# Go-ahead products issued one at a time, the last expert's rows of x2 two steps sooner, sigmoid's table loaded by itself, and two planner costs

## The chip, the cores and the metric

The kernel runs on one core of a Trainium2 chip. The metric is the device time of one execution in microseconds (us), and the median of several executions is quoted. Five engines run their own instruction streams in order and meet at semaphores: TensorE (PE in the rows; PEld is its weight load), VectorE (DVE), ScalarE (ACT), GpSimd (POOL) and SyncE (SP), which issues most DMAs.

## What is computed

Three layers follow each other. Attention over 16 heads of 768 tokens lets a query see only keys of its own cluster. A mixture of 8 experts gives every token to the expert that its gate chooses. A feed-forward layer with a softplus-tanh gate works on the result, whose products are made of fp16 high and low parts so that the sums keep fp32 quality.

```python
def _attn_ref(q, k, v, centroids):
    ...
    mask = q_assign[:, :, :, None] == k_assign[:, :, None, :]
    scores = scale * np.matmul(q, k.transpose(0, 1, 3, 2))
    scores = np.where(mask, scores, -1000000000.0)
    ...
    return np.matmul(attn, v)

def _moe_ref(x, w_gate, w1, w2, capacity):
    logits = x @ w_gate
    expert_idx = np.argmax(logits, axis=1)
    ...
    h = np.maximum(np.einsum('ecd,edf->ecf', disp, w1), 0.0)
    y = np.einsum('ecf,efd->ecd', h, w2)
    ...
        out[i] = gate_w[i] * y[expert_idx[i], pos[i]]

def _moe2_ref(x, w_in, w_out):
    h = x @ w_in
    sp = np.where(h > 20.0, h, np.log1p(np.exp(np.minimum(h, 20.0))))
    g = h * np.tanh(sp)
    return g @ w_out
```

## The kernel before

The program is one straight line of instructions. Its order is not written by hand: a list planner (class `Plan`) keeps a calendar for every engine, gives each operation the first gap on its engine after its inputs are due, and issues all operations in the order of their planned starts. A planned duration is a number in the code; it decides order, and nothing else. `plan.best` lets the planner choose between two engines (VectorE or ScalarE for a copy). `plan.dma` places transfers in a like manner: a load has a transfer time, and a DMA transpose has in addition a landing tail, `CFG["tm"]`.

The stages, with the times of the profiled execution:

- **0 to 229 us, attention.** `load` (L417 to L430) brings q, k and v in pieces of one or two heads (`qf`, `kf`, `vf`, two buffers each) through SP's queue. ScalarE and VectorE make `QK`, `KX`, `QX`, `VX`, `VW` of them; DMA transposes on SP's queue make `QKT` (L568), `KXT`, `QXT` (L673) and `Q` (L754). Cluster masks are written into `KX` and `QX` by L665 and L668 on ScalarE. Then come scores (L781, L782), exponentials `P` (L789) and the products with v (L833).
- **228 to 260 us, gate and go-ahead.** The last tokens' transposes (L1058) and gate products (L1046) end the gate. Counting products (L1148, L1269) give every token its slot; GpSimd writes the rows to their slots in DRAM. While this runs, TensorE computes the "go-ahead" part: a fixed number of columns (112 and 80) of two experts whose rows need no slot. `go_ahead` has `first()` for the first layer: for the first of the two experts the products are fp32 (`phv`, L1722, `xw` by the weights in `xd` or `w1f`), for the second they are fp16 (L1719). Each `f` needs four fp32 products, one for each `kk`; they were planned as two operations of two products.
- **260 to 403 us, the experts.** Products L1572 and L1621. `weigh` makes each expert's rows of the feed-forward input, `yg` (L1675), `x2h` (L1678, ScalarE) and `x2l` (L1681). For the last expert the step that makes `x2h` and `x2l` is kept (`rest`) and is planned later, at feed-forward step number `lasti`.
- **403 to 660 us, feed-forward.** The work is cut into 32 steps (half of the tokens, 128 of the 2048 hidden columns). An H step is two blocks of 384 tokens, with 12 products each (L1924: `x2h` and `x2l` by `winh` and `winl`); an O step is six blocks of 3 products of 512 columns (L2012: `po` += `gt` by the weights in `xd`). Between H and O, `hs` is copied out of PSUM (L1941 on ScalarE, L1943 on VectorE), and `active` forms `gt`: exp (L1965), min (L1968), ln (L1971), z (L1974), sigmoid (L1977), g (L1980), high part (L1984), low part (L1987). Exp and ln share one activation table, sigmoid needs another, so every group loads two tables on ScalarE (ACT_TABLE_LOAD at L1964 and L1977). The H steps form groups: the first two and the last two groups hold one H step (`m == 1`), the others two. The weights arrive in fp32 (`w2s`) and are rounded and split in pieces of 512 columns (`wis`, L1826 to L1838; `winh` L1841; `winl` L1844; or into `xd`) between these operations.

The last expert's rows of x2 go to an offset that is known only at run time. So every H block that is issued behind a copy of them waits for that copy, and each copy waits for the H blocks issued ahead of it, whichever tokens they read.

The sums `po` have a PSUM bank each; the first six H blocks borrow those banks, and the later ones take turns in two banks `fh`, so that an H block waits until the `hs` of the last block but one has left its bank.

Of the kernel before, what the change touches and what calls it, by code (L numbers as in the profile page):

```python
# [48 lines left out]
    sbias=1000.0, plsl=30000, nl=1, abias=-20000.0, ol=2, oh=3, mbias=1500.0, glate=0.5, vpool=1000.0, wa=4, wb=4,   # L49
    vz=81, vs=1, hsbias=500.0, obias=1000.0, nwi=4, nw=2, avw=225, fli=44, rsl=6000.0, lag0=5, lags=(), lasti=6, idl=30000, ask=2, pli=12, ob=4, pr=1.0, pr0=1.0, nwo=3, wo0=40, wos=8, hsl=200.0, ps=4, rn=5, rs=3, gl0=3, gsp=1500.0, tm=600.0, lmg=200.0, ht=400.0, hbl=1300.0, warm=4700,  # L50
)
# [205 lines left out]
def act(n):  # L257
    return 0.834 * n + 95
# [5 lines left out]
def pe32(n):  # L264
    return max(n / 0.6, 224.0)


def dve1(n):
    return 1.042 * n + 68
# [14 lines left out]
def pe(n):  # L284
    return n / 2.4


class Builder:
# [102 lines left out]
    def attention(self, ctx, rctx, pctx, plan, mkeep, extra, then, exact=False):  # L391
# [24 lines left out]
        def load(i, n, nm):  # L416

            src = {"qf": q, "kf": k, "vf": v}[nm].rearrange("b h s d -> (b h) s d")

            def emit():  # L420
                t = prep.tile([128, 2, NT, D], F32, tag=nm, name=nm, bufs=P["ldb"])
                nc.sync.dma_start(
                    out=t[:, 0:n].rearrange("p h (n t) d -> p (h n) (t d)", t=3),
                    in_=src[i:i + n].rearrange("h (n p t) d -> p (h n) (t d)", n=BLK, t=3))
                for j in range(n):
                    st[nm, i + j] = t[:, j]
            x = Buf(nm, P["ldb"])
            for j in range(n):
                bf[nm, i + j] = x
            plan.dma("SP", 835 * n, emit, new=x)  # L430

# [913 lines left out]
    def second_half(self, plan, profile, xs, idc, before, free, mkeep=None):  # L1345
# [355 lines left out]
        def go_ahead():  # L1701
# [5 lines left out]
            def first(r, q):  # L1707
# [4 lines left out]
                def mm(f, k):  # L1712
                    def emit():
# [3 lines left out]
                        if half:  # L1717
                            for kk in range(KD):
                                nc.tensor.matmul(t["p"][:, f % NQ], lhsT=w[k == 1][:, kk, f2], rhs=st["x", r][:, 2 * kk + (k == 2), 0:cr], start=(k == kk == 0), stop=(k == 2 and kk == KD - 1))  # L1719
                        else:  # L1720
                            for kk in range(2 * k, 2 * k + 2):
                                nc.tensor.matmul(t["p"][:, f % NQ], lhsT=w[:, kk, f2], rhs=st["xw", r][:, kk], start=(kk == 0), stop=(kk == KD - 1))  # L1722
                    return emit
# [11 lines left out]
                for f in range(q * NQ, (q + 1) * NQ):  # L1735
                    if ("W", r, f // FC, 0) not in st:
                        ahead(r, f // FC, 0)
                    for k in range(3 if half else 2):
                        new = f % NQ == k == 0
                        plan.op("PE", KD * pe(cr) if half else 2 * pe32(cr), mm(f, k), use=(*st["W", r, f // FC, 0], *(st["X", r] if half else (st["XW", r],)), *(() if new else (b,))), new=b if new else None, add=b)  # L1740
                plan.op("ACT", act(NQ * cr) + 55, relu, use=b, new=ht)
# [210 lines left out]
        def active(t, hs, m):  # L1952
# [20 lines left out]
            def z_():  # L1973
                V.tensor_tensor(out=flat(t["u"]), in0=flat(t["u"]), in1=flat(t["hs"]), op=ALU.add)  # L1974

            def sig_():
                A.activation(out=flat(t["u"]), in_=flat(t["u"]), func=AF.Sigmoid)  # L1977
# [12 lines left out]
            end = plan.op("ACT", act(n) + 93, ln_, use=u, add=u)  # L1990
            TABLE.writers = {"ACT": end}
            plan.op("DVE", dve1(n), z_, use=(u, hs), add=u)
            end = plan.op("ACT", act(n) + LOAD, sig_, use=(u, TABLE), add=u)
            TABLE.writers = {"ACT": end}
# [369 lines left out]
```

## Time and profile before

| what | value |
|---|---|
| median of 3 executions (lowest, highest) | 663.39 us (661.07, 667.71) |
| profiled execution: its time, its span | 667.3 us, 665.2 us |
| mean granted TensorE clock | 0.987 |
| TensorE busy | 628.2 us, 94% |
| VectorE busy | 540.9 us, 81% |
| ScalarE busy | 487.2 us, 73% |
| GpSimd busy | 44.2 us, 7% |

A span runs from the first to the last instruction. The busy shares are means over stages: in each stage another engine may be the one that the others wait for. A row of the timeline has the start, the busy time, engine, line, operation, what is written and read, the number of instructions run together in the row and, in brackets, the idle time of the engine just ahead of it with what ended that idle time.

### The profile page before, as it was taken

The numbers are of one execution on the slowest core, as the hardware profiler recorded it, in microseconds if no ns is written. First come the engines' busy times: TensorE is split into PE (matmuls) and PEld (weight loads), VectorE is DVE, ScalarE is ACT, GpSimd is POOL, SyncE is SP. The second block draws the span as 40 slices with busy tenths as digits, with TensorE's granted clock in tenths as the row PEclk, the third lists the DMA queues.
The fourth block names the chain that finished last, engine by engine and source line by source line (L and its number), as shares of the span: only waits on it lengthen the run. The fifth ranks groups of instructions, "written<-read, shape, count | busy, mean of one in ns | idle before, by whom it ended". The sixth has DMA issues, their size and how long they took to land. (4 is left out here: it accounts for less than half of the span.)

```text
span 665.2 us, 15340 instructions
## 1 busy us (share of the span) xinstructions
PE 628.2 (94%) x6091; PEld 452.6 (68%) x6091; DVE 540.9 (81%) x1038; ACT 487.2 (73%) x738; POOL 44.2 (7%) x97
## 2 busy tenths in 40 slices
PE   7889999899998989999999899979999999999994
PEld 5668777687777878789999886545555555555542
DVE  8899999999897828988989896999888788545452
ACT  5699999687796325675777775998988888666760
POOL 4000000000500030000000000000000000001203
PEclk9999999999997989999999999999999999999998
DMA  7978789896796689998899991322213121000102
GB/s 204 174 153 220 201 177 231 173 238 120 173 152 178 197 284 287 295 301 261 246 269 279 286 311 33 102 88 73 86 36 93 63 96 34 1 0 17 80 0 99
DMA packets 149957, 104.96 MB, mean 158 GB/s; under 512 B 91764, under 2 KB 132725, under 8 KB 149877
## 3 DMA queue, kind: packets, MB, share of 16 engines
q1 hardware_dynamic: 147956, 97.22, 56.4%
q0 software_dynamic: 1920, 6.69, 2.7%
q8 instruction: 49, 0.80, 0.5%
q14 instruction: 32, 0.25, 0.1%
HBM read 68.21 MB, written 14.36 MB: 124 GB/s over the span
## 5 line engine op out<-in xcount | busy, mean ns | idle before, releaser
L2012 PEld LDWEIGHTS <-gt 128*128 128x128 f16 x576 | 56.4, 98 | 64.9
L789 ACT ACTIVATE P<-s 128x768 f32<-128x768 f32 x96 | 77.9, 812 | 28.4 <-PE s L782 26.7
L2012 PE MATMUL po<-xd,gt 128*128 128x512 f16 x432 | 97.3, 379 | 0.0
L1621 PE MATMUL py<-ht,wh 128*128 128x176 f16 (+6 forms) x768 | 79.1, 251 | 0.7 <-DVE wh L1454 0.6
L1572 PE MATMUL ph<-xt,wh 128*128 128x176 f16 (+6 forms) x756 | 76.1, 250 | 3.1 <-DVE wh L1454 2.1
L1924 PE MATMUL fh<-x2l,winh 128*128 128x384 f16 x232 | 75.6, 326 | 1.9 <-DVE x2l L1681 1.9
L1924 PE MATMUL fh<-x2h,winh 128*128 128x384 f16 x232 | 75.6, 326 | 1.4 <-ACT hs L1941 1.4
L1924 PEld LDWEIGHTS <-winh 128*128 128x128 f16 x512 | 50.1, 98 | 38.2 <-issue 2.3
L1924 PE MATMUL fh<-x2h,winl 128*128 128x384 f16 x232 | 75.6, 326 | 0.0
L716 ACT ACTIVATE ev<-pm 128x768 f16<-128x768 f32 x87 | 70.3, 811 | 1.4 <-PE pm L707 1.4
L1572 PEld LDWEIGHTS <-wh 128*128 128x128 f16 x768 | 63.8, 98 | 8.5 <-DVE wh L1454 2.5
L781 PE MATMUL s<-Q,KXT 81*128 81x384 f16 x192 | 63.3, 330 | 6.3 <-DMA Q<-QX 5.4
L1621 PEld LDWEIGHTS <-wh 128*128 128x128 f16 x768 | 63.7, 98 | 6.3 <-DVE wh L1454 1.5
L782 PE MATMUL s<-QKT 128*128 128x384 f16 x192 | 63.4, 330 | 0.0
L805 DVE TENSOR_TENSOR PL<-P 128x768 f16<-128x768 f32 x64 | 59.8, 950 | 1.5 <-ACT P L789 1.5
L833 PEld LDWEIGHTS pa<-VW,P 128*128 128x128 f32 x384 | 54.7, 193 | 5.4 <-DVE rpm L1151 0.7
L833 PE MATMUL pa<-VW,P 128*128 128x65 f32 x384 | 56.5, 270 | 0.6 <-DVE rpm L1151 0.6
L707 PE MATMUL pm<-KXT,QXT 80*128 80x384 f16 x192 | 46.7, 329 | 4.3 <-ACT P L789 2.2
L833 PE MATMUL pa<-VX,P 128*128 128x65 f16 x768 | 48.6, 194 | 0.0
L833 PEld LDWEIGHTS <-P 128*128 128x128 bf16 x768 | 47.3, 105 | 0.0
L833 PE MATMUL pa<-VX,PL 128*128 128x65 f16 x384 | 45.3, 192 | 0.0
L1595 ACT ACTIVATE ht<-ph 128x176 f16<-128x176 f32 (+6 forms) x63 | 21.2, 336 | 30.9 <-PE ph L1572 29.3
(268 smaller groups left out, 1247.7 us busy)
## 6 DMA issues: line engine op xcount, KB each, us to landing
w1f<-in_moe_w_dram SPq DMA_DIRECT2D x42, 512.0 KB
w2f<-in_moe_w_dram SPq DMA_DIRECT2D x32, 512.0 KB
w2s<-in_moe_w_in_dram SPq DMA_DIRECT2D x16, 512.0 KB
w2s<-in_moe_w_out_dram SPq DMA_DIRECT2D x16, 512.0 KB
xs<-zero SPq DMA_DIRECT2D x13, 576.0 KB
xd<-in_moe_w_dram SPq DMA_DIRECT2D x6, 512.0 KB
kf<-in_k_dram SPq DMA_DIRECT2D x7, 384.0 KB
qf<-in_q_dram SPq DMA_DIRECT2D x7, 384.0 KB
```

The source lines that it names most:

```text
L707: nc.tensor.matmul(pm[:, j, 0:384], lhsT=QXT[0:80, g], rhs=KXT[0:80, 3 * j:3 * j + 3].rearrange("c t p -> c (t p)"), start=True, stop=True)
L716: nc.scalar.activation(out=st["ev", u][:, t].rearrange("p (a c) -> p a c", a=2), in_=st["pm", u, t][:, :, 0:384], func=AF.Copy, scale=1.0 ...
L781: nc.tensor.matmul(s[:, j, 0:384], lhsT=KXT[0:81, kt], rhs=Q2[0:81].rearrange("c t p -> c (t p)"), start=True, stop=False)
L782: nc.tensor.matmul(s[:, j, 0:384], lhsT=QKT[:, 1, kt], rhs=QKT[:, 0, 3 * blk:3 * blk + 3].rearrange("c t p -> c (t p)"), start=False, stop ...
L789: nc.scalar.activation(out=st["P32", u, pr], in_=st["s", u, pr][:, :, 0:384], func=AF.Exp, scale=sc)
L805: nc.vector.tensor_tensor(out=st["PL", u][:, 2 * pr:2 * pr + n], in0=st["P32", u, pr][:, 0:n], in1=st["PH", u, pr][:, 0:n], op=ALU.subtract)
L833: nc.tensor.matmul(pa[:, t], lhsT=lhs, rhs=rhs, start=(n == 0), stop=(n == len(mm) - 1))
L1572: nc.tensor.matmul(st["p", i], lhsT=w[:, kk, fs], rhs=xt[:, 2 * kk + a], start=(kk == 0 and n == 0), stop=(kk == KD - 1 and n == 2))
L1595: nc.scalar.activation(out=t[:, 0], in_=st["p", i], func=AF.Relu)
L1621: nc.tensor.matmul(py, lhsT=w[:, f2, dsl], rhs=x, start=(f == 0 and j == 0), stop=(f == NF - 1 and j == 2))
L1924: nc.tensor.matmul(ph[b][:, 0:HB], lhsT=t2[w][:, f, k // 3], rhs=t2["x2"][x][:, k // 3, c0:c0 + HB], start=(k == 0), stop=(k == 3 * KD - 1))
L2012: nc.tensor.matmul(t2["o"][k], lhsT=gt[:, a, ts_], rhs=t2["wo"][f][:, w], start=(first and j == 0), stop=(last and j == 2))
```

## The change

Four edits are made.

1. The last expert's `x2h` and `x2l` are planned at feed-forward step 4 and no longer at step 6 (`lasti`).
2. The planner's landing tail of a DMA transpose is 900 ns and no longer 600 ns (`tm`). For a load of q, k or v of heads 0 to 3 it counts 640 ns a head and no longer 835 ns. Neither changes an instruction; both change planned starts.
3. In `first`, the fp32 go-ahead products are planned one by one, not in twos.
4. In `active`, for a group of one H step, sigmoid's table is loaded by an operation of its own right behind the ln, so that it no longer stands behind the sigmoid's wait for z.

```diff
@@ CFG
-    lasti=6,
+    lasti=4,
...
-    tm=600.0,
+    tm=900.0,
@@ load
-            plan.dma("SP", 835 * n, emit, new=x)
+            plan.dma("SP", (640 if i < 4 else 835) * n, emit, new=x)
@@ go_ahead, first
-                            for kk in range(2 * k, 2 * k + 2):
-                                nc.tensor.matmul(t["p"][:, f % NQ], lhsT=w[:, kk, f2], rhs=st["xw", r][:, kk], start=(kk == 0), stop=(kk == KD - 1))
+                            nc.tensor.matmul(t["p"][:, f % NQ], lhsT=w[:, k, f2], rhs=st["xw", r][:, k], start=(k == 0), stop=(k == KD - 1))
...
-                    for k in range(3 if half else 2):
+                    for k in range(3 if half else KD):
...
-                        plan.op("PE", KD * pe(cr) if half else 2 * pe32(cr), mm(f, k), use=(*st["W", r, f // FC, 0], *(st["X", r] if half else (st["XW", r],)), *(() if new else (b,))), new=b if new else None, add=b)
+                        plan.op("PE", KD * pe(cr) if half else pe32(cr), mm(f, k), use=(*st["W", r, f // FC, 0], *(st["X", r] if half else (st["XW", r],)), *(() if new else (b,))), new=b if new else None, add=b)
@@ active
+            def table():
+                A.preload_act_table_set("sigmoid_and_others")
...
+            early = m == 1
+            if early:
+                end = plan.op("ACT", LOAD, table, use=(u, TABLE))
+                TABLE.writers = {"ACT": end}
             plan.op("DVE", dve1(n), z_, use=(u, hs), add=u)
-            end = plan.op("ACT", act(n) + LOAD, sig_, use=(u, TABLE), add=u)
+            end = plan.op("ACT", act(n) + (0.0 if early else LOAD), sig_, use=(u, TABLE), add=u)
```

Since planned starts change, the order changes on most engines. Three places matter below.

**TensorE at the end of the gate.** Before, the last transposes of the gate (L1058) are followed by the gate products (L1046), and the first eight fp32 go-ahead products (`phv`) stand behind the last of these. Before:

```order
L1058 LDWEIGHTS xd [waits DVE_49]
L1058 MATMUL pm<-ident,xd 128x128
...
L1046 LDWEIGHTS XTb [waits Activation_49]
L1046 MATMUL pm<-WG,XTb 128x8 [waits DVE_49]
...
L1722 MATMUL phv<-xw,xd 128x112 [waits PE_49]
L1722 MATMUL phv<-xw,xd 128x112 x7
L1148 LDWEIGHTS tri
L1148 MATMUL pm<-OH,tri 128x24 [waits DVE_49]
```

Now (the line numbers of the new kernel are lower by one here):

```order
L1721 MATMUL phv<-xw,xd 128x112 [waits DVE_49,PE_49]
L1058 LDWEIGHTS xd [waits Activation_49]
...
L1721 MATMUL phv<-xw,xd 128x112
L1058 LDWEIGHTS xd [waits DVE_49]
...
L1721 MATMUL phv<-xw,xd 128x112
L1046 LDWEIGHTS XTb [waits DVE_49]
L1046 MATMUL pm<-WG,XTb 128x8 [waits Activation_49]
...
L1721 MATMUL phv<-xw,xd 128x112 x8
L1148 LDWEIGHTS tri
L1148 MATMUL pm<-OH,tri 128x24 [waits DVE_49]
```

Four single go-ahead products have moved ahead: one between the two halves of the transposes, one after the next three transposes, one after the last three, one between the two sets of nine gate products. The first of them waits for VectorE to have read the bank that it writes. Eight go-ahead products still stand ahead of the counting products L1148, as before; behind these come four, then L1269, then eight and eight.

**ScalarE at the start of the feed-forward layer**, from the second single group's ln on. Before:

```order
L1971 ACTIVATE u<-u,one 128x768 [waits DVE_49]
L1826 ACTIVATE wis<-w2s 128x512 [waits DMAHW7_49,Activation_49]
L1941 ACTIVATE hs<-fh_7811 128x384 [waits PE_49]
L1977 ACT_TABLE_LOAD
L1977 ACTIVATE u<-u 128x768 [waits DVE_49]
L1841 ACTIVATE winh<-wis 128x512 [waits DVE_49]
L1941 ACTIVATE hs<-fh_7812 128x384 [waits PE_49]
L1984 ACTIVATE gt<-u 128x768 [waits DVE_49]
L1826 ACTIVATE wis<-w2s 128x512 [waits DMAHW0_49,DVE_49]
L1941 ACTIVATE hs<-fh_7997 128x384 [waits PE_49]
```

Now:

```order
L1970 ACTIVATE u<-u,one 128x768 [waits DVE_49]
L1976 ACT_TABLE_LOAD
L1979 ACTIVATE u<-u 128x768 [waits DVE_49]
L1940 ACTIVATE hs<-po_7824 128x384 [waits PE_49]
L1825 ACTIVATE wis<-w2s 128x512 [waits DMAHW7_49,Activation_49]
L1986 ACTIVATE gt<-u 128x768 [waits DVE_49]
L1940 ACTIVATE hs<-fh_7818 128x384 [waits PE_49]
L1793 TENSOR_LOAD meta
...
L1678 ACTIVATE x2h<-yg 128x144 [waits PE_49]
```

The table load follows the ln at once, the sigmoid follows it, and the two copies that stood ahead of the sigmoid (`wis`, `hs`) stand behind it. The last expert's four `x2h` copies (L1678), of which one is shown, come directly behind an `hs` of the eighth H block; before, they stood behind the exp and the ln of the first group of two. On TensorE the first H block that waits for them is now the second of those behind the first eight; before, it was the sixth. Three of the six O blocks of the second single group now stand ahead of that H block, and a fourth behind it.

**SP's queue at the start**, from the load of heads 1 and 2 on. Before:

```order
L422 DMA kf<-in_k_dram 128x4x192 [waits DMAHW1_49,DVE_49]
L568 DMA_TRANSPOSE QKT<-QK 128x12x128 [waits DMAHW0_49,DVE_49]
L422 DMA qf<-in_q_dram 128x4x192 [waits DMAHW2_49]
L422 DMA vf<-in_v_dram 128x4x192 [waits DMAHW3_49]
L568 DMA_TRANSPOSE QKT<-QK 128x12x128 [waits DVE_49,Activation_49]
```

Now:

```order
L422 DMA kf<-in_k_dram 128x4x192 [waits DMAHW1_49,DVE_49]
L422 DMA qf<-in_q_dram 128x4x192 [waits DMAHW2_49,DMAHW0_49,DVE_49]
L422 DMA vf<-in_v_dram 128x4x192 [waits DMAHW3_49,DVE_49,Activation_49]
L568 DMA_TRANSPOSE QKT<-QK 128x12x128 [waits DVE_49]
L568 DMA_TRANSPOSE QKT<-QK 128x12x128 [waits DVE_49,Activation_49]
```

The loads of q and v of heads 3 and 4 have gone ahead of head 1's first transpose. On ScalarE, in the same stretch, the two mask copies of head 0 (L665 and L668), which stood between two `VX` copies, now stand behind that pair, two `VW` copies (L584) and a `KX` and a `QX` copy (L553).

## Rows read from the trace of the kernel before

**Rows 1.** The page, busy time, share of the span and instructions of each engine

```profile
PE 628.2 (94%) x6091; PEld 452.6 (68%) x6091; DVE 540.9 (81%) x1038; ACT 487.2 (73%) x738; POOL 44.2 (7%) x97
```

**Rows 2.** Windows: length, then busy time (and instructions) by engine, granted clock, DMA share, GB/s

```profile
0.00:50.00 50.00, 42.30 (x476) 30.61 (x477) 44.55 (x109) 36.75 (x76) 7.43 (x59) 1.00 0.81 177
...
450.00:650.00 200.00, 200.00 (x1071) 104.60 (x1070) 140.91 (x163) 155.21 (x163) 7.40 (x6) 1.00 0.15 48
```

**Rows 3.** Timeline of TensorE, start of the feed-forward layer

```profile
425.11 0.33 PE L1924 MATMUL fh<-x2h,winh 128*128 128x384 f16 x1
...
437.73 0.32 PE L1924 MATMUL fh<-x2l,winh 128*128 128x384 f16 x1 [0.61 <-DVE x2l L1681]
...
440.66 0.32 PE L1924 MATMUL fh<-x2l,winh 128*128 128x384 f16 x1 [1.30 <-DVE x2l L1681]
...
444.53 0.32 PE L1924 MATMUL fh<-x2h,winh 128*128 128x384 f16 x1 [1.44 <-ACT hs L1941]
```

**Rows 4.** Timeline of ScalarE in the same stretch

```profile
419.84 0.94 ACT L1971 ACTIVATE u<-u,one 128x768 f32<-128x768 f32 x1
...
421.75 1.28 ACT L1977 ACT_TABLE_LOAD   x1
423.04 0.84 ACT L1977 ACTIVATE u<-u 128x768 f32<-128x768 f32 x1
...
442.61 1.48 ACT L1965 ACTIVATE u<-hs 128x1536 f32<-128x1536 f32 x1
444.00 0.47 ACT L1941 ACTIVATE hs<-fh 128x384 f32<-128x384 f32 x1
```

**Rows 5.** Timeline of VectorE in the same stretch

```profile
425.79 0.96 DVE L1987 TENSOR_TENSOR gt<-u,gt 128x768 f16<-128x768 f32 x1 [0.31 <-ACT gt L1984]
...
437.37 0.75 DVE L1681 TENSOR_TENSOR x2l<-yg,x2h 128x144 f32 x3
438.03 1.75 DVE L1980 SCALAR_TENSOR_TENSOR u<-hs,u 128x1536 f32<-128x1536 f32 x1
...
440.30 0.30 DVE L1681 TENSOR_TENSOR x2l<-yg,x2h 128x144 f32 x1
```

**Rows 6.** Timeline of TensorE at the end of the gate

```profile
229.14 0.73 PE L1058 MATMUL pm<-ident,xd 128*128 128x128 f16 x6 [0.47 <-ACT xd L869]
230.11 0.37 PE L1046 MATMUL pm<-WG,XTb 128*128 128x8 f16 x9 [0.23 <-DVE XTb L1066]
231.10 0.37 PE L1046 MATMUL pm<-WG,XTb 128*128 128x8 f16 x9 [0.62 <-ACT XTb L1066]
231.32 3.65 PE L1722 MATMUL phv<-xw,xd 128*128 128x112 f32 x16
...
235.19 2.02 PE L1722 MATMUL phv<-xw,xd 128*128 128x112 f32 x16
...
244.46 0.30 PE L1719 MATMUL phv<-xv,wh 128*128 128x80 f16 x4 [1.18 <-issue]
```

**Rows 7.** Windows of TensorE there: length, its busy time, granted clock, DMA share, GB/s

```profile
230.00:231.50 1.50, 0.77 (x19) 0.97 1.02 310
231.50:234.50 3.00, 3.00 (x15) 0.50 0.94 358
```

**Rows 8.** Timeline of ScalarE at the start

```profile
6.31 0.42 ACT L575 ACTIVATE VX<-vf 128x256 f16<-128x256 f32 x1 [1.17 <-DMA vf<-in_v_dram]
...
9.93 0.94 ACT L537 ACTIVATE QK<-qf 128x384 f16<-128x384 f32 x2 [0.68 <-DMA qf<-in_q_dram]
...
11.91 0.27 ACT L665 ACTIVATE KX<-eg 128x96 f16<-128x96 f16 x1
...
16.75 0.52 ACT L537 ACTIVATE QK<-qf 128x384 f16<-128x384 f32 x1 [1.36 <-DMA qf<-in_q_dram]
```

**Rows 9.** Timeline of SP's DMA queue at the start

```profile
11.07 1.40 SPq L568 DMA_TRANSPOSE QKT<-QK  x1
12.53 0.56 SPq L422 DMA_DIRECT2D qf<-in_q_dram  x1
```

More of the change, by code (lines that the diff above doesn't have):

```diff
@@ L49 @@
     sbias=1000.0, plsl=30000, nl=1, abias=-20000.0, ol=2, oh=3, mbias=1500.0, glate=0.5, vpool=1000.0, wa=4, wb=4,
-    vz=81, vs=1, hsbias=500.0, obias=1000.0, nwi=4, nw=2, avw=225, fli=44, rsl=6000.0, lag0=5, lags=(), lasti=6, idl=30000, ask=2, pli=12, ob=4, pr=1.0, pr0=1.0, nwo=3, wo0=40, wos=8, hsl=200.0, ps=4, rn=5, rs=3, gl0=3, gsp=1500.0, tm=600.0, lmg=200.0, ht=400.0, hbl=1300.0, warm=4700,
+    vz=81, vs=1, hsbias=500.0, obias=1000.0, nwi=4, nw=2, avw=225, fli=44, rsl=6000.0, lag0=5, lags=(), lasti=4, idl=30000, ask=2, pli=12, ob=4, pr=1.0, pr0=1.0, nwo=3, wo0=40, wos=8, hsl=200.0, ps=4, rn=5, rs=3, gl0=3, gsp=1500.0, tm=900.0, lmg=200.0, ht=400.0, hbl=1300.0, warm=4700,
 )
```

## The prediction, made before the changed kernel had run

> **What bounds the kernel now.** I read the page first: TensorE is busy 94% of the span, VectorE 81%, ScalarE 73% [rows 1]. A mean does not say who is waited for, so I went to the windows of 50 us. In the first one VectorE is busy 44.55 us and TensorE 42.30; neither is full, and VectorE has more to do. From 450 to 650 us TensorE is busy for the whole 200.00 us [rows 2]. So in the tail no edit can gain anything that does not take work off TensorE, and none does: the number of products is the same. What can be gained lies ahead of 450 us, where TensorE has gaps; and whatever is gained there comes out at the end in full, because the tail is one block of products that starts earlier.
>
> So I looked at the timeline of TensorE where the change moves something. At the start of the feed-forward layer there are three gaps: 0.61 and 1.30 us, both ended by `x2l` on VectorE, and 1.44 us, ended by an `hs` copy on ScalarE [rows 3]. That is 3.35 us. At the end of the gate there are gaps of 0.47, 0.23 and 0.62 us, 1.32 us together, each ended by a copy on ScalarE or VectorE; then come eight fp32 go-ahead products (sixteen records, two for each) that take 3.65 us, while the next eight take 2.02 us at 235.19 [rows 6]. The windows say why: the granted clock is 0.97 up to 231.5 us, and 0.50 from there to 234.5 us [rows 7]. These are the two levels, 2.4 and 1.2 GHz, and the fall comes behind the stretch with the gaps, in which TensorE was busy 0.77 of 1.50 us.
>
> **The feed-forward start: last expert's x2 sooner, table loaded apart.** The two edits belong together. The `x2l` of the last expert comes late, since VectorE runs three of them at 437.37, then an operation of 1.75 us (g, L1980) and only at 440.30 the fourth [rows 5]; TensorE has by then asked twice. In the new order these copies stand some 10 us earlier, behind the eighth H block's `hs`, where the neighbours are operations of the single groups, half as long. The H blocks that wait for them (second and third behind the first eight) have four O blocks and one O block ahead of them as cover. I count no stall of `x2l` there. So 0.61 + 1.30 = 1.91 us go away.
>
> What is late next? First, the O blocks of the second single group have moved up: TensorE asks for them at about 425.11 us, which is where the second H block started before [rows 3]. Their input ended at 425.79 + 0.96 = 426.75 us [rows 5]. The early table load makes this up in part. Before, the ln ended at 419.84 + 0.94 = 420.78, an `hs` copy and a `wis` copy followed, the table was loaded at 421.75 and the sigmoid ran at 423.04 [rows 4]. With the load right behind the ln, the sigmoid can start at 420.78 + 1.28 = 422.06, which is 0.98 us sooner; the input is then ready at about 425.8, and a stall of 0.7 us stays. The table load costs ScalarE nothing more, since it is the same load at another place.
>
> Here a rule of the Trainium skill would give another sum. The rows show a table load of 1.28 us whose sigmoid starts 0.01 us behind its end [rows 4]; nothing else is lost. The page "ScalarE: Activation LUTs" (What ACT_TABLE_LOAD costs) states about 1283 ns for the load, which agrees, and about 1380 ns of drain on top, 2.66 us in all for every switch, which these rows do not show. If the drain were there and went under cover with the load, the input would be ready 1.38 us sooner still, the stall of 0.7 us would be gone, and the forecast would be 659.6 us.
>
> Second, the third gap. In the trace of before the H block at 444.53 us waits for an `hs` copy that ScalarE starts at 444.00 us, behind an exp of 1.48 us that began at 442.61 [rows 4]. In the new order the pair of blocks two places further on (the fourth behind the eight) waits in the same way, behind a table load and the same exp: I put down 1.1 us, between nothing and the 1.44 of the row, and 0.5 us for the block behind it. The stalls left are 0.7 + 1.1 + 0.5 = 2.3 us against 3.35. **Term: -1.1 us.** Its bounds are -3.35 (all three gaps gone) and +1.2 (the stalls left are twice as long as I put down, 4.6 us).
>
> The early table load for the last two single groups, near 650 us, is worth nothing: TensorE is full there.
>
> **Single go-ahead products.** Four of the 32 fp32 products now stand in the gaps of the gate. A product at full clock costs 2.02 / 8 = 0.25 us [rows 6]; four make 1.0 us, and the gaps have 1.32 us. If they only fill gaps, TensorE reaches what comes behind 1.0 us sooner. Three things can take some of it back. The first single waits for VectorE to have left its bank, and everything behind it on TensorE would wait with it; its bank is due ahead of 229.14 us, when TensorE was idle for the copy `xd` anyway. The second and third stand ahead of transposes whose inputs may already be there, so they delay the chain transposes, XTb, gate, counting by up to 0.25 us each. The counting products (L1148) still stand behind eight go-ahead products as before.
>
> The larger part is the clock. If the filled gaps keep it from falling at 231.5 us, the eight products take 2.02 us and not 3.65 us: 1.63 us more. The row speaks for it: the level falls behind the stretch in which TensorE was half idle, and the singles fill most of that. The full gain is 1.0 + 1.63 = 2.6 us; taking off some 0.6 us for the delayed transposes, **term: -2.0 us**, bounds -2.6 and +0.5 (the clock falls as before and the singles delay the gate). A part of the gaps here stays: at 244.46 us TensorE idles 1.18 us for nothing the profile names (issue) [rows 6], and the new order leaves that work as it is. If such gaps hang on the transfers that run then, they may swallow some of what was gained.
>
> **The planner's two costs.** They move work at the start. Loads of heads 3 and 4 go out before head 1's transpose, which was issued at 11.07 us, and `qf` at 12.53 us behind it [rows 9]. Gain: ScalarE waited 1.36 us for that `qf` at 16.75 us [rows 8]. Loss: a two-head load takes (9.93 - 6.31) / 2 = 1.8 us of the DMA engines, for between these two starts on data two such loads landed [rows 8], and head 1's transpose now runs behind two more of them, up to 3.6 us later. And head 0's masks, at 11.91 us before [rows 8], have five more copies ahead of them, some 1.5 us. Attention follows VectorE's sum of work, which is the same (44.55 of 50 us there), so a late head costs only what VectorE has not in hand from another head. Gain and loss are of one size: **term: 0**, bounds -1.4 and +3.6. Elsewhere the two costs swap neighbours in attention; I saw nothing that ends a wait of TensorE or VectorE: 0, bounds half a microsecond either way.
>
> **Sum.** -1.1 - 2.0 + 0 = -3.1 us on the profiled execution's 667.3 us, of which the span is 665.2: 664.2 us. That execution is 3.9 us above the median of the runs, 663.39, near the highest of them, 667.71; I take the difference to the median: 663.39 - 3.1 = 660.3 us.
>
> **The rivals.**
> - *The clock falls anyway.* Singles of 0.25 us leave shares of idle time in that stretch, and the wait for XTb stays. Then only the 1.0 us of filled gaps is left: -1.1 - 1.0 = -2.1, 661.3 us. A rule speaks for neither; only the row of the clock does, and it is one fall.
> - *The feed-forward stall only moves.* The last gap is ScalarE's, which is as busy as before; if the `hs` copies behind exp and table loads cost 3.35 us in their new places, that term is 0, and 661.4 us remain.
> - *Everything comes through.* All three gaps gone, clock held, the wait for `qf` gone: -3.35 - 2.6 - 1.4 = -7.35, 656.0 us.
> - *Slower: the start.* The start puts work for later heads ahead of what the first heads wait for; head 0's masks 1.5 us later and head 1's transpose 3.6 us cost 5.1 us if attention has nothing in hand. It decides from 3.1 us on, where it outweighs the two gains: 663.39 + 5.1 - 3.1 = 665.4 us. Against it: TensorE and VectorE both have idle time in the first window [rows 2], which a late head can be caught up in.
> - *Nothing that counts.* The gaps at the gate hang on transfers and the stall moves: 663.4 us.
>
> **How the numbers follow.** Forecast 0.42; clock falls 0.16; the stall only moves 0.12; everything 0.10; start slower 0.13; nothing 0.07. A measurement of this kernel cannot tell 1% (6.6 us) from no change. Below 656.8 us lies most of the case in which everything comes through and a little of the forecast's edge: 0.11. Above 670.0 us the slower case would need its loss doubled: 0.05. The range reaches from 656.0, where everything comes through, to 666.0, just beyond the slower case.
>
> **What would show it.** Right: no gap ended by `x2l` behind 430 us; sigmoid's table load right behind the ln with the sigmoid at its end; four single `phv` rows of about 0.25 us between 228 and 231 us; granted clock near 1.00 where it was 0.50 from 231.5 to 234.5 us; the last stall of TensorE ahead of the full stretch shorter. Wrong: the clock at 0.50 behind the singles; stalls of more than 2.3 us ended by `hs` between 425 and 446 us; the first `P` of head 0 and the end of attention later by some microseconds.

## The result, and the profile of the changed kernel

The changed kernel takes 657.10 us (median of 6 executions, 653.39 to 660.12), the kernel before 664.84 us (median of 6 beside it, 661.07 to 667.71). The ratio is 0.9882, with a 95% interval from 0.9834 to 0.9931: 0.7% to 1.7% faster. The prediction was 660.3 us, 0.5% faster, with a range from 656.0 to 666.0. The time lies in the range and the sign is right; the gain, 7.8 us by the ratio, is two and a half times the 3.1 us of the sum. Gains of the runs below are given in the same way, from the ratio of each kernel to the kernel before on its chip. The profiled execution of the changed kernel took 658.58 us, with a span of 656.4 us.

The page's first part and two windows of the changed kernel; the columns are those of [rows 1, 2]:

```profile
PE 627.3 (96%) x6097; PEld 451.4 (69%) x6097; DVE 541.6 (83%) x1044; ACT 485.3 (74%) x733; POOL 43.5 (7%) x96
...
0.00:50.00 50.00, 44.22 (x489) 32.53 (x490) 45.53 (x112) 37.51 (x77) 7.20 (x59) 1.00 0.77 176
...
450.00:642.00 192.00, 192.00 (x1027) 100.33 (x1026) 138.12 (x163) 148.21 (x152) 7.42 (x7) 1.00 0.15 47
```

TensorE's work is the same (627.3 us against 628.2) and the tail is as full as before; the span is shorter because TensorE idles less ahead of it.

Timeline of TensorE at the start of the feed-forward layer, which answers to [rows 3]. These are all of its idle times between the layer's first product at 397.75 us and the end of the full stretch:

```profile
426.78 0.32 PE L1923 MATMUL fh<-x2h,winh 128*128 128x384 f16 x1 [0.29 <-ACT hs L1940]
...
429.33 0.32 PE L1923 MATMUL fh<-x2h,winh 128*128 128x384 f16 x1 [0.44 <-ACT hs L1940]
```

No wait for `x2l` is left, and 0.73 us of idle time stands where 3.35 us stood. ScalarE and VectorE in the same stretch, for the second single group, which answer to [rows 4, 5]:

```profile
414.00 1.28 ACT L1976 ACT_TABLE_LOAD   x1
415.30 0.84 ACT L1979 ACTIVATE u<-u 128x768 f32<-128x768 f32 x1
```

```profile
418.04 0.96 DVE L1989 TENSOR_TENSOR gt<-u,gt 128x768 f16<-128x768 f32 x1
```

The table load stands behind the ln, the sigmoid at its end; `gt` is ready at 419.00 us.

Timeline of TensorE at the end of the gate, which answers to [rows 6], and its windows, which answer to [rows 7]:

```profile
227.41 0.45 PE L1721 MATMUL phv<-xw,xd 128*128 128x112 f32 x2 [0.16 <-DVE LG L1039]
...
227.89 0.43 PE L1721 MATMUL phv<-xw,xd 128*128 128x112 f32 x2
...
229.67 0.37 PE L1046 MATMUL pm<-WG,XTb 128*128 128x8 f16 x9 [0.31 <-ACT XTb L1066]
229.90 2.02 PE L1721 MATMUL phv<-xw,xd 128*128 128x112 f32 x16
...
253.23 0.97 PE L1572 MATMUL phl<-xt,wh 128*128 128x320 f16 x6 [1.68 <-DMA xt<-xs]
254.78 0.97 PE L1572 MATMUL phl<-xt,wh 128*128 128x320 f16 x6 [0.58 <-DMA xt<-xs]
```

```profile
226.30:229.90 3.60, 3.13 (x63) 1.00 0.95 311
229.90:232.90 3.00, 3.00 (x44) 1.00 0.86 301
```

The singles stand in the gaps, the eight products behind them take 2.02 us, and the clock stays at its upper level. The idle times named issue, of which [rows 6] shows one, are missing. New is the wait ahead of the first expert: TensorE now waits 2.3 us for `xt`, the first expert's rows, which GpSimd has dispatched to DRAM and SP's queue transposes back.

Each trace below splits into three stretches: from the start to the first product of the gate's last `pg` (L1046; `pg` below), from there to the first feed-forward product (`po`), and from there to the end of the span. "Dispatch" is the time from `pg` to the first row dispatch of GpSimd, "xt" from `pg` to the issue of the first expert's transposes, "issue" the sum of the idle times named issue among the fp16 go-ahead products. The first two lines are the traces of the result; the other kernels are those of the next section. The runs e1 to e4 were made on one chip, e5 to e8 on a second, e9 to e12 on a third; on which chips the first two traces were taken is not on record.

| trace | pg at | pg to po | po to end | dispatch | xt | issue |
|---|---|---|---|---|---|---|
| before | 227.7 | 176.0 | 261.5 | 9.6 | 25.0 | 3.1 |
| changed | 226.3 | 171.5 | 258.7 | 8.3 | 22.5 | none |
| e1 singles only | 226.5 | 175.8 | 261.6 | 8.2 | 23.2 | 3.7 |
| e2 x2 and table only | 224.2 | 175.4 | 258.2 | 9.9 | 24.5 | 2.6 |
| e3 costs only | 224.5 | 175.3 | 262.1 | 9.7 | 24.2 | 2.6 |
| e4 before again | 230.7 | 176.0 | 261.3 | 9.5 | 25.1 | 3.2 |
| e5 changed again | 227.7 | 173.4 | 258.3 | 8.2 | 22.6 | none |
| e6 all but singles | 224.8 | 172.8 | 258.4 | 9.3 | 23.2 | none |
| e7 x2 sooner only | 228.2 | 176.3 | 260.9 | 9.6 | 25.1 | none |
| e8 table apart only | 224.0 | 176.3 | 261.4 | 9.6 | 25.1 | none |
| e9 fillers, no singles | 226.8 | 174.7 | 261.4 | 8.2 | 23.8 | 3.0 |
| e10 tail only | 227.5 | 174.4 | 261.5 | 8.2 | 23.5 | 3.0 |
| e11 loads only | 225.1 | 176.0 | 261.4 | 9.5 | 25.1 | 3.5 |
| e12 feed weights later | 222.4 | 175.5 | 258.4 | 8.2 | 23.3 | 3.9 |

The last stretch is the steady one: 260.9 to 262.1 us wherever the two feed-forward edits are not both made, 258.2 to 258.7 us wherever they are. The first stretch differs by up to 8 us between the traces, and by 3 us between two executions of one program (before: 227.7 and 230.7).

Two things of the middle stretch are needed to read it. First, the experts behind the first `xt` product take 143.1 to 143.4 us up to `po` in the seven traces that have the idle times named issue and no singles. Second, in e5, e7 and e8 the clock falls to its lower level for 6.8 us at the first expert; in the changed kernel's first trace and in e6 it does not.

### The profile page after: what moved, and what is told of

Read it like the earlier page. It is cut to its first block, busy times and chain, and to the rows that moved or that the text cites. A ratio compares the mean times of both kernels' runs of the same rounds, so it can differ in the third digit from the quotient of the medians.

```text
span 656.4 us, 15358 instructions
## 1 busy us (share of the span) xinstructions
PE 627.3 (96%) x6097; PEld 451.4 (69%) x6097; DVE 541.6 (83%) x1044; ACT 485.3 (74%) x733; POOL 43.5 (7%) x96
## 5 line engine op out<-in xcount | busy, mean ns | idle before, releaser
L1572 PEld LDWEIGHTS <-wh 128*128 128x128 f16 x768 | 63.9, 98 | 10.8 <-DVE wh L1454 4.1
L1454 DVE SCALAR_TENSOR_TENSOR wh<-w1f,wh 128x1024 f16<-128x1024 f32 x32 | 38.9, 1217 | 3.4 <-ACT wh L1446 3.4
```

What stands on the lines that cost most here:

```text
L1454: nc.vector.scalar_tensor_tensor(out=t["l"], in0=t["f"], scalar=SW, in1=t["h"], op0=ALU.mult, op1=ALU.subtract)
L1572: nc.tensor.matmul(st["p", i], lhsT=w[:, kk, fs], rhs=xt[:, 2 * kk + a], start=(kk == 0 and n == 0), stop=(kk == KD - 1 and n == 2))
```

## The experiments

My theory at the start was that three gains add up: the feed-forward start (-2.9 us in the two profiles), the stretch from gate to feed-forward (-4.5 us), attention (-1.4 us). The rivals were that the gate's gain belongs to the idle times named issue, which the change does not touch, and that parts of it were chance of one execution. So first each edit alone.

**e1, the single products alone.** The edit is the diff's third part by itself:

```diff
-                            for kk in range(2 * k, 2 * k + 2):
-                                nc.tensor.matmul(t["p"][:, f % NQ], lhsT=w[:, kk, f2], rhs=st["xw", r][:, kk], start=(kk == 0), stop=(kk == KD - 1))
+                            nc.tensor.matmul(t["p"][:, f % NQ], lhsT=w[:, k, f2], rhs=st["xw", r][:, k], start=(k == 0), stop=(k == KD - 1))
...
```

> The kernel before with the single go-ahead products alone (edit 3). My theory: the gaps of the gate are filled, the granted clock stays near 1.00 from 231.5 to 234.5 us, TensorE reaches the fp16 go-ahead products some 2.5 us sooner, and the idle times of 3.1 us named issue between 242 and 246 us are gone as well, because they hang on how TensorE's stream stands against what runs beside it; then the experts wait some 2 us for xt. Time 2 to 5 us under before, the feed-forward stalls as before (3.3 us). Rival: those idle times were an accident of one execution, or hang on the planner's costs; then 1.0 to 2.6 us under before.

Measured: 664.78 us, ratio 0.9984 (0.9952 to 1.0015). The clock held as expected and the eight products took 2.02 us, but the idle times named issue came all the same, 3.7 us of them. Timeline of TensorE, e1:

```profile
238.94 0.34 PE L1719 MATMUL phv<-xv,wh 128*128 128x80 f16 x5 [0.46 <-issue]
240.38 0.23 PE L1719 MATMUL phv<-xv,wh 128*128 128x80 f16 x2 [1.10 <-issue]
...
243.24 3.25 PE L1719 MATMUL phv<-xv,wh 128*128 128x80 f16 x49 [1.11 <-issue]
```

They end at 243.24 us, 2.1 us behind the start of the last row dispatch (`pg` at 226.46, last dispatch 14.67 us later). In before it was 243.78 and 245.92, again 2.1 us. So most of what TensorE gains ahead of them it loses in them: the first expert's first product starts 31.0 us behind `pg`, against 32.8 in before. These 1.8 us are lost again in the experts, which take 144.8 us up to `po` and not 143.2, among them waits for `yg` that before does not have:

```profile
310.19 0.76 PE L1621 MATMUL py<-ht,wh 128*128 128x224 f16 x6 [0.49 <-DVE yg L1675]
...
389.78 0.54 PE L1621 MATMUL py<-ht,wh 128*128 128x144 f16 x6 [0.38 <-DVE yg L1675]
```

My expectation that the singles end the idle times was wrong, and the time does not tell the singles from no change.

**e2, the two feed-forward edits alone.**

```diff
-    lasti=6,
+    lasti=4,
...
+            def table():
+                A.preload_act_table_set("sigmoid_and_others")
...
+            early = m == 1
+            if early:
+                end = plan.op("ACT", LOAD, table, use=(u, TABLE))
+                TABLE.writers = {"ACT": end}
...
-            end = plan.op("ACT", act(n) + LOAD, sig_, use=(u, TABLE), add=u)
+            end = plan.op("ACT", act(n) + (0.0 if early else LOAD), sig_, use=(u, TABLE), add=u)
```

> The kernel before with the last expert's x2 at step 4 and the table load apart (edits 1 and 4). My theory: the feed-forward layer alone gets shorter, its TensorE stalls fall from 3.35 to about 0.7 us, time 2.5 to 3 us under before, the gate as before with the clock at 0.50. Rival: the two edits move other work too, and the gain differs by more than 1 us from that.

Measured: 660.70 us, ratio 0.9949 (0.9920 to 0.9979), 3.4 us. The stretch behind `po` is 258.2 us against 261.3 in e4, and its idle times are those of the changed kernel (0.29 and 0.44 us). The theory stands: this is the one part whose gain is shown by time and trace alike.

**e3, the planner's two costs alone.**

```diff
-    tm=600.0,
+    tm=900.0,
...
-            plan.dma("SP", 835 * n, emit, new=x)
+            plan.dma("SP", (640 if i < 4 else 835) * n, emit, new=x)
```

> The kernel before with the planner's two costs alone (edit 2). My theory: attention ends 1 to 1.5 us sooner, nothing else moves, time 1 to 1.5 us under before. Rival: the order that these costs make also ends the idle times named issue between 242 and 246 us, and the time is 3 us or more under before.

Measured: 663.81 us, ratio 0.9974 (0.9948 to 1.0001), 1.7 us. It is at the edge of what the interval tells; the idle times named issue were there (2.6 us), so the rival falls. The trace's `pg` at 224.5 us would suit the theory, but e2, whose attention is that of before, has 224.2.

**e4, before again.**

> The kernel before once more, for a second trace. My theory: the clock falls to 0.50 again behind the gate's gaps and the idle times named issue near 242 to 246 us are there again within 1 us of the 3.1 us of the first trace. Rival: they are gone or are elsewhere, so that they belong to one execution and not to the kernel.

Measured: 670.02 us in this one execution. The clock fell again, and the idle times named issue were there with 3.2 us in the same place. So they do not belong to one execution. But its attention ended 2.9 us later than in the first trace, with the same program: a difference of 1.4 us in `pg` says nothing.

**e5, the changed kernel again**, and on another chip.

> The changed kernel once more, for a second trace and on the same chip as the runs below. In five traces of other kernels the idle times named issue among the fp16 go-ahead products add up to 2.6 to 3.7 us and end 2.1 us behind the start of the last of the six row dispatches of GpSimd; the first trace of the changed kernel had none. My theory: they are missing again, because with the changed order these products meet the dispatches otherwise; the stretch from the end of attention to the first feed-forward product takes 171 to 172 us as in its first trace, against 175.3 to 176.0 in the others; about 7 us under before. Rival: they come and go between executions; then this trace has 2.5 us or more of them and that stretch takes 174 us or more, and the gain comes from elsewhere.

Measured: 658.14 us, ratio 0.9889 (0.9837 to 0.9941). No idle time named issue; but e6 to e8, on the same chip, had none either, and two of these have the go-ahead products in the order of before. So the theory falls: it is not the change that removes them. The traces e5 to e8 (one chip) have none, the traces e1 to e4 and e9 to e12 (two chips) all have them. Where they are missing, TensorE reaches the first expert early and waits for `xt` in every trace. Timeline and windows of TensorE, e5:

```profile
255.11 1.30 PE L1572 MATMUL phl<-xt,wh 128*128 128x320 f16 x6 [2.12 <-DMA xt<-xs]
256.75 1.76 PE L1572 MATMUL phl<-xt,wh 128*128 128x320 f16 x6 [0.33 <-DMA xt<-xs]
```

```profile
253.20:257.20 4.00, 1.76 (x8) 0.80 0.97 211
257.20:261.20 4.00, 2.95 (x12) 0.50 1.01 344
```

Behind this wait the clock fell to its lower level; in the first trace of the changed kernel, after a like wait, it did not. That is most of the difference between 173.4 and 171.5 us: 1.5 us of it lie behind the first `xt` product (146.0 and 144.5 us to `po`).

**e6, all but the singles**: the changed kernel with this part undone.

```diff
...
-                    for k in range(3 if half else KD):
+                    for k in range(3 if half else 2):
...
```

> The changed kernel with the go-ahead products in twos as before (edit 3 undone). My theory: the single products are worth 2 to 3 us beside the other edits, so this kernel is 4.5 to 6 us under before, with the clock at 0.50 behind the gate's gaps and the idle times named issue back. Rival: they are worth 1 us, as they were alone, and the time is within 1 us of the changed kernel's.

Measured: 659.04 us, ratio 0.9927 (0.9896 to 0.9957), 4.9 us. Against e5 on the same chip the singles are worth 0.9 us by the medians and 2.5 us by the ratios (0.9889 and 0.9927), whose intervals overlap. So this does not decide between the theory (2 to 3 us) and the rival (1 us). The clock was at 0.58 behind the gate's gaps, near the 0.50 of the theory; the idle times named issue, which the theory had back, were missing. The middle stretches (172.8 us here, 173.4 in e5) do not settle it either, since the clock fell at the first expert in e5 and not here.

**e7, x2 sooner alone, and e8, the table apart alone.** They are the two halves of e2's diff.

> The kernel before with the last expert's x2 at step 4 alone. My theory: the waits for x2l go, but without the early table the second single group's gt is late by up to 1 us or the next hs wait takes part of it back; 1.5 to 2.5 us under before. Rival: it is worth the whole 3 us and the early table nothing.

> The kernel before with sigmoid's table loaded by itself in the single groups, alone. My theory: nobody waits for the second single group's gt in the order of before, so the time stays within 1 us of before, and the x2l waits of 1.9 us and the hs wait of 1.4 us stay within 0.7 us. Rival: the sooner gt lets the planner move the rest by itself, and 1.5 us or more are gained.

Measured: e7 664.56 us, ratio 0.9988 (0.9953 to 1.0023); e8 664.65 us, ratio 1.0001 (0.9966 to 1.0036). Neither shows a gain alone that its interval can tell; together they show 3.4 us (e2). Timeline of TensorE, e7:

```profile
426.62 0.61 PE L2012 MATMUL po<-xd,gt 128*128 128x512 f16 x2 [0.54 <-ACT gt L1984]
427.62 2.98 PE L2012 MATMUL po<-xd,gt 128*128 128x512 f16 x13 [0.39 <-DVE gt L1987]
...
435.90 0.32 PE L1924 MATMUL fh<-x2h,winh 128*128 128x384 f16 x1 [0.75 <-ACT hs L1941]
...
444.64 1.04 PE L2012 MATMUL po<-xd,gt 128*128 128x512 f16 x4 [0.35 <-DVE gt L1987]
...
446.01 0.32 PE L1924 MATMUL fh<-x2h,winh 128*128 128x384 f16 x1 [0.34 <-ACT hs L1941]
```

And e8:

```profile
434.45 0.32 PE L1924 MATMUL fh<-x2l,winh 128*128 128x384 f16 x1 [0.78 <-DVE x2l L1681]
...
437.38 0.32 PE L1924 MATMUL fh<-x2l,winh 128*128 128x384 f16 x1 [1.30 <-DVE x2l L1681]
...
441.25 0.32 PE L1924 MATMUL fh<-x2h,winh 128*128 128x384 f16 x1 [1.43 <-ACT hs L1941]
```

With x2 sooner alone the waits for `x2l` go, and waits for the second single group's `gt` (0.93 us) and for the next `gt` and `hs` (1.44 us) come: 2.4 us in place of 3.35. With the table apart alone `gt` is sooner, but TensorE meets the same `x2l` waits as before. The theory of e7 was right in its mechanism and too high in its price (1.5 to 2.5 us expected, 1.0 us of idle time less); that of e8 was right.

**e9, fillers without singles**: four products of ones by zeros in the places of the singles, overwritten by the first go-ahead product.

```diff
...
+                        for j in range(fillers if f % NQ == k == 0 else 0):
+                            plan.op("PE", 200, dummy(j), use=(*st["W", r, 0, 0], st["XW", r], *((b,) if j else ())), new=None if j else b, add=b)
...
```

> The kernel before with four idle matmuls of 448 columns (ones by zeros, overwritten afterwards) in the gate's gaps where the changed kernel has its four single go-ahead products; the go-ahead products stay in twos, nothing is moved and no result changes. It tells the clock from the moved work. My theory: the filled gaps keep the granted clock near 1.00, the eight go-ahead products behind them take 2.0 us and not 3.6, the first row dispatch stands 8.2 to 8.5 us behind the end of attention and not 9.5, and the time is 0.5 to 2 us under before, as with the singles. Rival: the clock falls to 0.50 all the same, the dispatch stays at 9.5 us, and the time is that of before.

**e10, the landing tail alone, and e11, the planned loads alone.**

> The kernel before with the planner's landing tail of transposes at 900 ns alone. On SP it moves one load of w1f (512 KB) ahead of the six transposes that end attention. My theory: the rows' dispatch then meets 512 KB less of loads, the first expert's transposes are issued 7.5 to 8.1 us behind the last dispatch and not 9.0, and where the experts wait for them the gain reaches the end: 1 to 2 us under before. Rival: that is hidden, and the time is within 0.7 us of before.

> The kernel before with the shorter planned loads of heads 0 to 3 alone. My theory: it moves work in the first 30 us only; gain and loss are of one size and attention ends within the spread of the traces of before (224 to 231 us); time within 0.8 us of before, the first expert's transposes 9.0 us behind the last dispatch. Rival: it is worth 1.5 us or more of the start.

Measured: e9 664.50 us, ratio 0.9993 (0.9963 to 1.0023); e10 666.30 us, ratio 1.0022 (0.9992 to 1.0053); e11 665.24 us, ratio 1.0013 (0.9982 to 1.0045). The windows of TensorE, each from `pg` to 3.6 us behind it and for 3 us more. e9:

```profile
226.84:230.44 3.60, 2.86 (x59) 1.00 1.02 306
230.44:233.44 3.00, 3.00 (x44) 1.00 0.96 355
```

e10:

```profile
227.54:231.14 3.60, 2.23 (x55) 1.00 0.65 204
231.14:234.14 3.00, 3.00 (x44) 1.00 0.83 300
```

e11:

```profile
225.10:228.70 3.60, 2.23 (x55) 1.00 0.94 304
228.70:231.70 3.00, 3.00 (x21) 0.53 0.87 321
```

With filled gaps (e9) the clock held; with open gaps it fell in e11 and held in e10, whose TensorE was busy for the same 2.23 us. Over all traces the clock held in 5 of 5 with filled gaps (changed, e1, e5, e9, e12) and fell in 8 of 9 with open ones. Wherever it held, the dispatch came at 8.2 to 8.3 us instead of 9.3 to 9.9. So the clock is what moves the dispatch, not the moved products: e9 moves none, and its rival, that the clock falls all the same, falls. But e9 gained nothing that its interval can show, and so did e10, in which two parts of the theory (clock and tail) came together: with the idle times named issue present, 1.3 to 1.6 us of the middle stretch (174.7 and 174.4 against 176.0) is all that was left.

e10's transposes were issued 8.8 us behind the last dispatch, where I expected 7.5 to 8.1. That says nothing for or against the tail, for they did not wait for the rows. On SP's queue they stand behind a load of w1f that waits for TensorE's first `pyv` products (L1763), and these stand behind the idle times. SP's queue in e10, its timeline and its longest wait from 235 to 260 us:

```profile
249.67 0.38 SPq L1441 DMA_DIRECT2D w1f<-in_moe_w_dram  x1
251.00 4.38 SPq L1415 DMA_TRANSPOSE xt<-xs  x2
```

```profile
SPq L1441 <- PE pyv L1763: 6.1, 1, 6.1
```

And in the changed kernel:

```profile
242.39 0.38 SPq L1441 DMA_DIRECT2D w1f<-in_moe_w_dram  x1
248.77 3.35 SPq L1415 DMA_TRANSPOSE xt<-xs  x2
```

```profile
SPq L1415 <- DMA xs<-xd,SLOT: 4.4, 1, 4.4
```

In all nine traces with idle times the transposes are issued 1.33 us behind this load, and no wait for the rows shows; in the five others they wait 2.6 to 4.8 us for the rows. So only these five tell when the rows land: with the load of w1f moved 7.5 to 7.9 us behind the last dispatch (e6, changed, e5), without it 9.1 (e7, e8). That agrees with the theory of e10, but in these traces the tail came together with the planned loads and the feed-forward edits. The gain of 1 to 2 us that I expected of e10 did not come. The theory of e11 stands: the shorter planned loads move nothing that can be measured.

**e12, two feed-forward loads later**: the changed kernel, in which the first two loads of `w2s` wait for the first expert's transposes.

```diff
-        **({"bias": P["obias"], "start": (FFN,)} if f >= P["nwi"] and mkeep is not None else {}))
+        **({"bias": P["obias"], "start": (FFN,)} if f >= P["nwi"] and mkeep is not None else {"start": st["X", nv]} if f < 2 else {}))
```

> The changed kernel with the first two loads of feed-forward weights (512 KB each), which are not used before 400 us, held back until the first expert's transposes. My theory: in the changed kernel TensorE waits 2.3 to 2.5 us for these transposes, which wait for the dispatched rows among 2 MB of loads; with 1 MB less they are issued 2 to 3 us sooner, the wait goes, and the time is 1 to 3 us under the changed kernel, 1.4 to 1.6% under before. Rival: the rows' landing is set by the dispatch itself; the transposes come as late as before and the time is that of the changed kernel.

Measured: 658.49 us, ratio 0.9928 (0.9896 to 0.9960). It does not beat the changed kernel (0.9882 and 0.9889, on other chips). It ran on a chip on which the idle times named issue are there (3.9 us), so TensorE came late to the first expert and had no wait for `xt` to lose. The transposes were issued 23.3 us behind `pg`, against 22.5 and 22.6 in the changed kernel; but here too that is 1.33 us behind the load of w1f that waits for TensorE. So this run does not decide whether the loads hold up the rows. Whether it helps on a chip without these idle times was not tried.

## Why the prediction was right, and where its sum was off

- *What bounds the kernel.* Right: the tail is full in both kernels, and what is gained ahead of 450 us arrives there whole in the feed-forward part (some 3.0 us less in the stretch behind `po` in five traces, 3.4 us less by the ratio of e2).
- *Feed-forward start, term -1.1 us.* The mechanism was right, the size not: the traces give -3.0 us, close to the outer bound of -3.35. The step that failed is the 2.3 us of stalls that I left. Measured are 0.29 and 0.44 us where I put 1.1 and 0.5, and nothing where I put 0.7 for `gt`. That one I had bounded by a sigmoid 0.98 us sooner. Counted from the layer's first product it is 17.55 us (415.30 - 397.75) against 19.36 (423.04 - 403.68), 1.81 us sooner: the two copies that stood ahead of the table load had moved behind it for the first group as well, and both gains add up. `gt` was ready at 419.00 us, 0.2 us before TensorE asked for it. The sum with the drain that the Trainium skill states ("ScalarE: Activation LUTs", What ACT_TABLE_LOAD costs), 659.6 us, came nearer to the result, but not for its reason: the table load took 1.28 us again and the sigmoid followed 0.02 us behind it, so no drain shows in this trace either.
- *That two edits belong together.* Right, and more so than the text said: of 3.35 us of stalls 2.37 are left in e7, 3.51 in e8 and 0.73 with both.
- *Singles and clock, term -2.0 us.* The clock held and the products took 2.02 us, as forecast (e1, e5 and e12 too). The price was wrong in its path. I took TensorE for the engine that sets the way from gate to experts, so that 1.0 + 1.6 us sooner would come out at the end. On that way TensorE ends in a wait: for `xt` where the idle times named issue are missing, and in these idle times, which end with the dispatches, where they are there. So little more than the 1.3 us by which the dispatches start sooner can come through: in e9, e10 and e1 the first expert starts 1.3 to 1.8 us sooner behind `pg`. In e1 the experts lose 1.6 us of it again, in e12, which has the singles too, 1.2 us; why is open. Alone the singles gave 1.1 us with an interval from a loss of 1.0 to a gain of 3.2 us, and in company 0.9 or 2.5 us, as medians or ratios are taken (e6 against e5).
- *The planner's costs, term 0.* At the start right: `load` alone gave a ratio of 1.0013 with an interval across 1 (e11), and head 0's first exponential came at 20.42 us against 19.62, so the loss that I named is there. The gain that I named is not: ScalarE's wait of 1.36 us for `qf` is gone, but it waits 1.00 us at 16.91 and 0.46 us at 18.31 for others. By 50 us TensorE and VectorE have done more work than before (44.22 and 45.53 us against 42.30 and 44.55), so the loss is caught up. What I did not see is that the tail moves a load of w1f out of the time in which the rows land. On one chip the `xt` transposes came 2.5 us sooner behind `pg` in the changed kernel (e5) than in e7 and e8, of which 1.3 us are the dispatch; the other 1.2 us go with this load, as in e6, but no run shows the tail alone as their cause. What that is worth is not shown: e6, with costs and without singles, needs 172.8 us from `pg` to `po`, where e7 and e8 need 176.3, but some 2.3 of these 3.5 us come behind the waits for `xt`, in the experts, where the clock fell in e7 and e8 and not in e6.
- *Sum.* On a chip without the idle times the parts are -3.0 (feed-forward) and -2.9 (e5 against e7 and e8, with the clock's fall at the first expert in all three), -5.9 us together. Measured on that chip (e5) are 7.4 us by the ratio (3.9 to 10.8) and 5.5 by the medians (658.14 and 663.68), and 7.8 us in the first measurement, whose trace lacks that fall. What attention adds cannot be told: `pg` stands at 224.0 to 230.7 us in the traces with before's costs or one of them, and at 222.4 to 227.7 in those with both.
- *The range.* At 657.1 us the result lies next to the rival in which everything comes through (656.0), but not for its reasons: of the gate's -2.6 some 1.3 us came through, the -1.4 at the start did not show, and what came in their place (the transposes sooner, the clock at the first expert) stands in no term. That the range held it is in part luck.
- *Open.* What the idle times named issue are, why two chips have them and one does not, and what the changed kernel gains on a chip that has them. e12, its nearest relative there, gained 0.7%, and its middle stretch is hardly shorter (175.5 us against 176.0).

Rows on ScalarE for the first exponential, in the timelines of before and of the changed kernel:

```profile
19.62 0.81 ACT L789 ACTIVATE P<-s 128x768 f32<-128x768 f32 x1
```

```profile
20.42 0.81 ACT L789 ACTIVATE P<-s 128x768 f32<-128x768 f32 x1 [0.57 <-PE s L782]
```

## What to carry to other kernels

Here two edits whose gains one by one stayed within the noise were worth 0.5% together, since each removed the wait that the other left or uncovered: after moving a late input forward, look for the wait that ends next and remove it in the same step. Before pricing time that an engine gains, follow that engine to its next wait; if that wait is ended by another chain (here gate, dispatch, DRAM, transposes), only what that chain gains comes through. Before reading a transfer's issue time as the landing of its input, see what stands ahead of it on its queue. Split several traces of the same program by stages before reading a difference of a stage: between two executions of the kernel before, the first stage differs by 3 us and the last by 0.2.

## What the runs showed of the hardware

Among the fp16 go-ahead products TensorE idled with nothing named as the cause, 2.6 to 3.9 us in nine traces. The starts after these idle times lie 0.7 us or 1.4 us apart (in e1 240.38, then 241.11, 241.82 and 243.24), and the last one comes 2.0 to 2.2 us behind the start of the last row dispatch of GpSimd. Five traces, four of them from one chip, have no such idle time with the same products beside the same dispatches: there these 96 products take 3.6 us from the first to the last, in the nine 6.9 to 9.6 us. The nine traces also hold fewer semaphore records (6963 to 6980 updates against 7152 to 7158), and most of the missing ones belong to the transfers that GpSimd issues; so a cause that was not recorded is not excluded.

In seven of these nine traces (all but e2 and e3) the clock falls to its lower level for 3.4 us among these products, in before at 245.1 us.

The clock's fall behind the gate's gaps is not sure: with 2.0 to 2.2 us of work in 3.60 us it fell in eight traces and held in one (e10). Four small products in these gaps held it each time.
